# A gated MLP after block-sparse attention: u and the spatial product computed with channels on partitions

## The chip, the cores and the metric

The kernel runs on one core of a Trainium2 chip. The metric is the device time of one execution in microseconds. A core has five engines that run side by side and meet through semaphores: PE (TensorE, the matrix multiplications; its weight loads are listed apart as PEld), DVE (VectorE), ACT (ScalarE), POOL (GpSimd) and SP (SyncE, which here issues nearly all DMAs, in order). Matrix products are written to tiles in PSUM; everything else lives in SBUF.

## The reference, cut to what matters

Block-sparse attention (4 batches, 8 heads, 768 positions, head size 64) makes x, and a gated MLP with a spatial product follows. The change touches the MLP and a few copies in the attention's setup.

```python
scores = scale * np.matmul(q, k.transpose(0, 1, 3, 2))
scores = np.where(mask, scores, -1e9)          # window, first and last block, 3 sampled blocks a row
attn = softmax(scores);  attn_out = np.matmul(attn, v)
x = attn_out.transpose(0, 2, 1, 3).reshape(B, S, H * D)          # (4, 768, 512)

h = np.maximum(x @ w_in, 0.0)                                    # (4, 768, 1024)
u, v = h[..., :512], h[..., 512:]
v_n = (v - mean(v)) / sqrt(var(v) + 1e-6)                        # over the 512 channels
v_s = np.einsum('ts,bsd->btd', w_spatial, v_n) + b_spatial[None, :, None]
out = (u * v_s) @ w_out                                          # (4, 768, 512)
```

## The kernel before

**Attention.** The work is cut into slots, written out by hand. In each slot PE makes the scores of one step (`qk_unit` in the first 36 slots, batch 0; `qk_full` in the 144 after them), ACT takes the exponential, and PE multiplies the exponentials of an earlier slot with v (`av_unit`, `av_full`, seven slots later). The mask is in the matmul: rows 64 to 95 of the tile `kq` hold, next to the 64 rows of each head's keys and queries, one-hot rows of the key's block and the query block's penalties. `rows` copies these from head 0 to others, and `mask_rows` makes the penalties by a small matmul of `bm`. In the setup one of the copies for head 2 (`rows(slice(2, 3), ...)`) is done by ACT (512 columns) and one by POOL (256). `filler` issues matmuls on a tile of zeros between the first real ones.

**MLP.** One `Moe` object per batch makes a list of steps, one matmul each, and `run_queue` deals them out over the slots: so many behind each slot's scores and attention products. `in_steps` are the products x w_in: per chunk of 128 positions (six, `tcc`) a `v_product` and a `u_product` of four matmuls, with 128 columns of `xt` (x transposed, channels on partitions) as weights and 512 columns of `w_in_t` streamed, so positions are on the output's partitions. v is normalised along its row: DVE takes statistics (`bn_stats`, `bn_aggr`), POOL makes `rstd` for a group of two or three chunks, and `vn_one` lets DVE normalise one chunk, at the earliest 9 steps after the group's statistics and then every second step. The spatial products (`s_product`, six matmuls) have blocks of `w_spt` as weights and stream `vn[:, s, :]` for s = 0 to 5; DVE reads the product from PSUM, adds the bias (`b_col`, one number per partition) and multiplies by u, in place in `un`, in one instruction. The output product needs the gated values with channels on partitions, so they are transposed: `dma_start_transpose` from SP into `gt`, two chunks at a time; for the last batch also one chunk at a time, and the last chunk on PE (`g_transpose`, four transposes and a DVE copy). `o_product` then has `gt` as weights and streams `w_out_t`; ACT or DVE copies the result to `osb`, and SP writes it out.

Batch 0's steps start in slots 16, 29 and 41, those of batches 1 and 2 where their last head ends, and those of batch 3 (`last`, the tail) run after the last slot with nothing between them; there `last_x` begins the products before the last x is complete. A product's PSUM bank comes from two (`moeA`, `moeB`) in turn; in the tail from six. Steps of one batch are in the order written, so what a step waits for on PE holds up all that follows it on PE.

The order of u and v products: `SEQ` for batches 1 and 2, a string in `last_x` for batch 3.

Of the kernel before, what the change touches and what calls it, by code (L numbers as in the profile page):

```python
# [10 lines left out]
FP32 = mybir.dt.float32  # L11
# [15 lines left out]
def kernel(  # L27
# [38 lines left out]
    FILL, FILL2, FILL3 = 26, (2, 2, 2), 3  # L66
# [12 lines left out]
    b_col = const.tile([128, NCH], FP32)  # L79
# [129 lines left out]
    def dve_copy(o, i):  # L209
        nc.vector.tensor_copy(out=o, in_=i)  # L210
# [76 lines left out]
    filler(FILL2[0], wps)  # L287
    mask_rows(psum.tile([128, 1024], FP32, tag="sc", bufs=2, name="mq"), 0, act_copy, 1)
    rows(slice(2, 3), slice(0, 512), nc.scalar)
    filler(FILL2[1], wps)  # L290
# [4 lines left out]
    filler(FILL2[2], wps)  # L295
    mask_rows(psum.tile([128, 512], FP32, tag=moe_tag(), bufs=1, name="mq"), 1, act_copy, rs=MR)
    split0(psq, 0, *Q4, 1)
    rows(H1, qcols(0, 2), PL)
    rows(slice(2, 3), slice(512, S), PL)
# [22 lines left out]
    nc.sync.dma_start(out=b_col, in_=moe_b_spatial.rearrange("(p c) -> p c", c=NCH))  # L322
# [198 lines left out]

    def ws_cast(i):
        if i % 2 == 0:
            ws["b", i // 2] = work.tile([128, 2, NCH, 128], BF16, tag="ws_b", bufs=2, name="ws_b")
        src = ws.pop(("f", i)).rearrange("p (s c) -> p c s", c=NCH)
        for c0 in range(0, NCH, NCH // 3):
            cs = slice(c0, c0 + NCH // 3)
            nc.gpsimd.tensor_copy(out=ws["b", i // 2][:, i % 2, cs], in_=src[:, cs])
# [36 lines left out]
    class Moe:  # L565
        def __init__(self, b):
            self.b, self.last = b, b == B - 1
            w = lambda nm: work.tile([128, NCH, DH], BF16, tag=nm, bufs=1, name=nm)
            self.un, self.vn = w("un"), w("vn")
            self.gt = work.tile([128, NCH, NDH, 128], BF16, tag="gt", bufs=1, name="gt")  # L570
            self.mv = work.tile([128, NCH, 2], FP32, tag="mv", bufs=2)
            self.std = work.tile([128, NCH], FP32, tag="std", bufs=2)
            self.rstd = work.tile([128, NCH], FP32, tag="rstd", bufs=2)
            self.vn_due = deque()
            self.steps = 0
# [36 lines left out]
        def u_product(self, tcc):  # L612
            def done(ps):
                if self.b == 0 and tcc in U_DVE:
                    ts(self.un[:, tcc, :], ps, 0.0, ALU.max)
                else:
                    nc.scalar.activation(out=self.un[:, tcc, :], in_=ps, func=AF.Relu)
            return product(NDM, lambda g: self.xt(g, tcc), lambda g: w_in_t[:, g, 0:DH],
                           self.last, done)

        def s_product(self, tcc):
            def done(ps):
                nc.vector.scalar_tensor_tensor(out=self.un[:, tcc, :], in0=ps,  # L623
                                               scalar=b_col[:, tcc:tcc + 1],
                                               in1=self.un[:, tcc, :], op0=ALU.add,
                                               op1=ALU.mult)
                if self.last and tcc == NCH - 1:
                    return
                if self.last and tcc == NCH - 2:
                    g0 = tcc  # L630
                elif tcc % 2 == 1:
                    g0 = tcc - 1
                else:
                    return
                nc.sync.dma_start_transpose(
                    out=self.gt[:, g0:tcc + 1].rearrange("p t c n -> p (t c) n"),
                    in_=self.un[:, g0:tcc + 1, :].rearrange("p t d -> p (t d)"))
            return product(NCH, lambda s: w_spt[:, tcc, s, :], lambda s: self.vn[:, s, :],
                           self.last, done)


        def g_transpose(self):
            ps = bank("ps_g", "av")
            for d in range(NDH):
                tr(ps, d, self.un[:, NCH - 1, d * 128:(d + 1) * 128])
            dve_copy(self.gt[:, NCH - 1].rearrange("p c n -> p (c n)"), ps[:, 0:NDH * 128])

        def o_product(self, tcc, n):
# [4 lines left out]
            for i in range(parts):  # L653
# [10 lines left out]
                steps += product(NDH, lambda d: self.gt[:, tcc, d, :],  # L664
# [9 lines left out]
        def rest_steps(self):  # L674
            out = []
            for tcc in range(NCH):
                out += self.s_product(tcc)
            first = out[0]
            out[0] = lambda: ([self.vn_one(True) for _ in range(NCH)], first())
            for n, tcc in enumerate((0, 1, 5, 2, 3, 4) if self.last else range(NCH)):  # L680
                out += self.o_product(tcc, n)
                if self.last and n == 1:
                    out.insert(len(out) - 3, self.g_transpose)
            return out
# [29 lines left out]
    ROWS = [(3, 2, 8, qcols(0)), (1, 3, 4, K_), (4, 4, 6, K_), (8, 6, 8, K_),  # L714
# [54 lines left out]
    def last_x():  # L769
# [4 lines left out]
        seq = m.in_steps("v0 v1 u0 v2 v3 v4 v5 u1 u2 u3 u4 u5", 3)  # L774
# [41 lines left out]
    for i, sl in enumerate((24, 30, 50)):  # L816
        when(sl, c(ws_tr, i))
    when(50, *[c(w_out_load, g) for g in range(NDH)])
# [61 lines left out]
```

## Time and profile before

| | |
|---|---|
| median of 3 runs | 210.97 us (210.81 to 211.08) |
| the profiled execution | 211.73 us, of which the span 209.9 us |
| setup, until ACT's exponentials run without a gap | 0 to 12.5 us |
| batch 0's attention (36 slots) | to about 47 us |
| batches 1 to 3's attention (144 slots), the MLP of batches 0 to 2 between | to about 182 us |
| the tail: MLP of batch 3 | 182 to 206.4 us, then the last write |

The profile lists each engine's busy time, the groups of instructions by line, operation and tiles, what each waited for, the chain that ended last, and timelines by engine with start and duration. Its times are those of one execution; matmuls are pipelined, so a group's mean duration (378 ns for 512 columns) is a latency, and the distance of two starts (216 ns) is what one costs in a row. A small part of the matmul records is missing from the trace.

### The profile page before, as it was taken

To read this page: it belongs to the slowest core of one execution; us is meant where nothing else is said; L and a number is where in the kernel's file an instruction comes from. 1 tells how busy PE (TensorE), PEld (TensorE's weight loads), DVE (VectorE), ACT (ScalarE), POOL (GpSimd) and SP (SyncE) were. 2 spreads that over 40 slices of the span, in tenths; PEclk is the share of its full clock that TensorE was granted. 3 is DMA by queue.
4 is the path that set the end of the run, shared out by engine and by line. 5 is a ranking of instruction groups with operands and counts; after the bars stand their busy time and mean duration, and the time that the engine had idled before them with its cause. 6 is when DMAs were issued, how large, how long until landed. Compare 5 with 4: busy or idle time off the path is not lost.

```text
span 209.9 us, 5319 instructions
## 1 busy us (share of the span) xinstructions
PE 201.3 (96%) x2106; PEld 129.1 (61%) x2140; DVE 136.4 (65%) x301; ACT 168.8 (80%) x222; POOL 83.3 (40%) x184
## 2 busy tenths in 40 slices
PE   8789999999999999999999999999999999999993
PEld 6569878766666666665566556665566556544441
DVE  7768987999874756484975454284985443476551
ACT  6979999999999999979998888979889787266021
POOL 6689869957828726006159051006220000012000
PEclk9999999999999999999999999999999999999998
DMA  5999799999999999999965497478501225610256
GB/s 162 330 357 344 222 314 285 251 301 359 250 338 188 264 165 296 270 219 345 210 216 112 116 247 179 153 177 262 102 3 35 53 53 116 222 54 0 50 146 228
DMA packets 64684, 41.96 MB, mean 200 GB/s; under 512 B 45716, under 2 KB 59412, under 8 KB 64660
## 3 DMA queue, kind: packets, MB, share of 16 engines
q1 hardware_dynamic: 64228, 41.24, 76.0%
q10 hardware_dynamic: 432, 0.39, 0.6%
q8 instruction: 16, 0.26, 0.5%
q14 instruction: 8, 0.07, 0.1%
HBM read 24.38 MB, written 6.29 MB: 146 GB/s over the span
## 4 chain that ended last, share of the span: by engine, by line
PE 87%; DMA 4%; DVE 2%; SPq 1%; ACT 1%; issue 1%; POOL 0%; ACTq 0%
PE ps_moe L555 31%; PE ps L421 22%; PE ps_av L469 13%; PE ps_t L555 7%; PE ps L408 6%; PE ps_av L451 4%; DMA st_k<-in_k_dram 4%; PE ps_sc L555 3%; PE ps L262 1%; SPq L108 1%; DVE kq L210 1%; ACT a_all L413 1%; DMA out_dram<-osb 1%; PE ps_av L262 1%; ACT osb L213 0%
## 5 line engine op out<-in xcount | busy, mean ns | idle before, releaser
L424 ACT ACTIVATE a_all<-ps 128x768 bf16<-128x768 f32 x144 | 113.7, 811 | 15.5 <-PE ps L421 7.2
L421 PE MATMUL ps<-kq 128*128 128x512 bf16 (+1 forms) x288 | 70.3, 325 | 0.2
L469 PEld LDWEIGHTS <-a_all 128*128 128x128 bf16 x864 | 46.6, 98 | 19.4
L469 PE MATMUL ps_av<-vv,a_all 128*128 128x65 bf16 x864 | 51.0, 194 | 0.1
L421 PEld LDWEIGHTS <-kq 128*128 128x128 bf16 x288 | 27.8, 97 | 30.1 <-issue 0.2
L555 PE MATMUL ps_moe<-w_in_t,xt 128*128 128x512 bf16 x128 | 39.4, 378 | 0.5
L413 ACT ACTIVATE a_all<-ps 128x1024 bf16<-128x1024 f32 x35 | 33.9, 1024 | 1.9 <-PE ps L408 1.4
L136 POOL CAST nat<-st_k 128x256 bf16<-128x256 f32 (+3 forms) x37 | 16.7, 482 | 42.9 <-DMA st_k<-in_k_dram 31.4
L555 PE MATMUL ps_moe<-vn,w_spt 128*128 128x512 bf16 x98 | 30.5, 378 | 0.6
L592 POOL TENSOR_SCALAR std<-mv 128x3 f32<-128x3 f32 (+1 forms) x9 | 2.1, 238 | 50.8 <-DVE mv L589 36.9
L408 PE MATMUL ps<-kq 88*128 88x256 bf16 (+1 forms) x136 | 21.0, 275 | 1.0 <-DVE kq L210 0.6
L623 DVE SCALAR_TENSOR_TENSOR un<-ps_moe,b_col,un 128x512 bf16<-128x512 f32 x18 | 13.5, 748 | 12.9 <-PE ps_moe L555 10.9
L555 PE MATMUL ps_moe<-w_out_t,gt 128*128 128x512 bf16 x66 | 20.2, 378 | 0.1
L555 PEld LDWEIGHTS <-xt 128*128 128x128 bf16 x192 | 15.2, 97 | 7.1 <-DVE xt L210 0.2
L433 DVE RECIPROCAL rc<-ps_av 128x6 f32<-128x6 f32 (+1 forms) x36 | 6.6, 184 | 19.9 <-PE ps_av L469 18.8
L434 DVE TENSOR_TENSOR xn<-ps_av,rc 128x384 bf16<-128x384 f32 (+1 forms) x36 | 18.5, 513 | 1.2
L136 POOL CAST nat<-st_q 128x256 bf16<-128x256 f32 (+2 forms) x41 | 17.2, 447 | 3.9 <-DMA st_q<-in_q_dram 3.6
L136 POOL CAST vv<-st_v 128x256 bf16<-128x256 f32 (+1 forms) x36 | 17.4, 516 | 3.1 <-DMA st_v<-in_v_dram 3.0
L588 DVE BATCH_NORM_STATS2 stats<-vn 128x6 f32<-128x512 bf16 x24 | 16.5, 688 | 1.5 <-ACT vn L583 0.9
L184 DVE TENSOR_SCALAR vn<-ps_moe 128x512 bf16<-128x512 f32 x18 | 12.3, 683 | 6.0 <-PE ps_moe L555 6.0
L451 PE MATMUL ps_av<-vv,a_all 128*128 128x65 bf16 x288 | 14.6, 194 | 1.0 <-POOL vv L136 1.0
L451 PEld LDWEIGHTS <-a_all 128*128 128x128 bf16 x288 | 13.5, 98 | 2.7 <-issue 1.5
(92 smaller groups left out, 215.5 us busy)
## 6 DMA issues: line engine op xcount, KB each, us to landing
st_v<-in_v_dram SPq DMA_DIRECT2D x16, 384.0 KB, 6.0
out_dram<-osb SPq DMA_DIRECT2D x23, 256.0 KB, 2.4
st_k<-in_k_dram SPq DMA_DIRECT2D x15, 384.0 KB, 4.4
st_q<-in_q_dram SPq DMA_DIRECT2D x12, 384.0 KB, 4.9
ws_f<-in_moe_w_spatial_dram SPq DMA_DIRECT2D x6, 384.0 KB, 4.7
w_f<-in_moe_w_in_dram SPq DMA_DIRECT2D x8, 256.0 KB, 5.6
w_f<-in_moe_w_out_dram SPq DMA_DIRECT2D x4, 256.0 KB, 5.6
st_q<-in_q_dram SPq DMA_DIRECT2D x3, 256.0 KB, 6.9
```

The source lines that it names most:

```text
L136: eng.tensor_copy(out=dst, in_=src)
L184: nc.vector.tensor_scalar(out=out, in0=in0, scalar1=s1, scalar2=s2, op0=o0, **kw)
L408: nc.tensor.matmul(out=ps[:, at:at + n * TW], lhsT=kq[0:KR, h, ci * 128:(ci + 1) * 128], rhs=kq[0:KR, h, qcols(t0, n)], start=True, stop=True)
L413: nc.scalar.activation(out=out, in_=ps, func=AF.Exp, scale=0.125)
L421: nc.tensor.matmul(out=ps[:, n0:n1], lhsT=kq[:, j % H, ci * 128:(ci + 1) * 128], rhs=kq[:, j % H, S + n0:S + n1], start=True, stop=True)
L424: nc.scalar.activation(out=a_ref["h", j][:, ci, :], in_=ps[:, 0:S], func=AF.Exp, scale=0.125)
L434: nc.vector.tensor_tensor(out=out, in0=ps[:, :, 0:D], in1=rc[:, 0:n].to_broadcast([128, n, D]), op=ALU.mult)
L451: nc.tensor.matmul(out=av_ref[u][:, to, :], lhsT=a_ref[u][:, at:at + 128], rhs=vv[pp % NVV][:, h, ci, :], start=(ci == 0), stop=(ci == NCH ...
L469: nc.tensor.matmul(out=av_ref[j][:, qc, :], lhsT=a_ref["h", j][:, ci, qc * 128:(qc + 1) * 128], rhs=vv[p % NVV][:, h, ci, :], start=(ci == ...
L555: nc.tensor.matmul(out=ref["ps"][:, 0:w], lhsT=lhs(i), rhs=rhs(i), start=(i == 0), stop=(i == n - 1))
L588: nc.vector.bn_stats(out=stats, in_=self.vn[:, tcc, :])
L623: nc.vector.scalar_tensor_tensor(out=self.un[:, tcc, :], in0=ps, scalar=b_col[:, tcc:tcc + 1], in1=self.un[:, tcc, :], op0=ALU.add, op1=AL ...
```

## The change

The u product and the spatial product swap their two operands. u: 128 columns of `w_in_t` (channels) are the weights and `xt` (positions) is streamed; spatial: 128 channels of `vn[:, s, :]` are the weights and the rows of `w_spt` are streamed. Both results then have channels on partitions. Each product fills one bank of 512 numbers, as an area of `nd` blocks of channels by `n` chunks of positions: for u in batch 0 two blocks by two chunks; in the other batches two blocks by the first two chunks (products 0, 1) and one block by the last four (2 to 5); for the spatial products one block by the first four chunks (0 to 3) and two blocks by the last two (4, 5). With nd = 2 a product is made of twice as many matmuls of 256 columns, two to a step; the number of steps is the same. `un` holds the gated values as [channel, block of channels, position] and is the output product's weights itself; `gt`, its transposes and `g_transpose` are gone, and the last batch's output chunks run in order.

The bias now runs along the free dimension: `b_load` brings it on SP in slot 46 as a broadcast to all 128 partitions (the small load of `b_col` in the setup goes), a DVE copy in slot 52 puts it in the order of the chunks (`b_row`), and the eviction is two DVE instructions, an add into the float32 tile `sb` and a multiply by u.

The last batch's order of products is v0 v1 v2 u0 ... instead of v0 v1 u0 v2 ...; in the setup, four fillers stand behind both mask products in place of two at each of three places, and head 2's key rows are copied by DVE in slot 0 instead of by ACT and POOL ahead of it.

```diff
@@ -63,7 +63,7 @@
     TC = NCH // NT
     TW = TC * 128
     S0 = NT * NG * 3
-    FILL, FILL2, FILL3 = 26, (2, 2, 2), 3
+    FILL, FILL2, FILL3 = 26, 4, 3
     U_DVE = (0, 1, 2, 3, 4, 5)
 
     const = ctx.enter_context(tc.tile_pool(name="const", bufs=1))
@@ -76,7 +76,7 @@
     w_in_t = const.tile([128, NDM, DFF], BF16)
     w_out_t = const.tile([128, NDH, DM], BF16)
     w_spt = const.tile([128, NCH, NCH, 128], BF16)
-    b_col = const.tile([128, NCH], FP32)
+    b_row = const.tile([128, S], FP32)
     mhalf = const.tile([128, NCH], FP32)
 
     kq = const.tile([128, H, 2 * S], BF16, name="kq")
@@ -284,19 +284,15 @@
     ps0 = bank()
     head(ps0, 0, *K4)
     split0(ps0, 0, *K4, 0)
-    filler(FILL2[0], wps)
     mask_rows(psum.tile([128, 1024], FP32, tag="sc", bufs=2, name="mq"), 0, act_copy, 1)
-    rows(slice(2, 3), slice(0, 512), nc.scalar)
-    filler(FILL2[1], wps)
     psq = bank("psq", "av")
     head(psq, 0, *Q4)
     split0(psq, 0, *Q4, 0)
     split0(ps0, 0, *K4, 1)
-    filler(FILL2[2], wps)
     mask_rows(psum.tile([128, 512], FP32, tag=moe_tag(), bufs=1, name="mq"), 1, act_copy, rs=MR)
+    filler(FILL2, wps)
     split0(psq, 0, *Q4, 1)
     rows(H1, qcols(0, 2), PL)
-    rows(slice(2, 3), slice(512, S), PL)
 
     ORDER = ("k1 q1a v0 k2 q2a v1 k3 q3a v2 q1b q2b r v3 q3b q0c w00 w01 w02 w03 w10 w12 w11 w13").split()
     PIECE = {"k": ALLC, "v": ALLC, "a": C01, "b": C25, "c": C45, "q": ALLC}
@@ -319,7 +315,6 @@
             rows(slice(2, 4), qcols(1), PL)
         for y in ORDER[i + AHEAD:i + AHEAD + 1]:
             ahead(y)
-    nc.sync.dma_start(out=b_col, in_=moe_b_spatial.rearrange("(p c) -> p c", c=NCH))
 
     def second():
         ps2 = bank("ps2", "av")
@@ -519,6 +514,10 @@
         nc.sync.dma_start(out=ws["f", i],
                           in_=moe_w_spatial.rearrange("(p c) s -> c p s", c=NCH)[i])
 
+    def b_load():
+        ws["b_nat"] = work.tile([128, S], FP32, tag="ws_f", bufs=6, name="b_nat")
+        nc.sync.dma_start(out=ws["b_nat"], in_=moe_b_spatial.partition_broadcast(128))
+
     def ws_cast(i):
         if i % 2 == 0:
             ws["b", i // 2] = work.tile([128, 2, NCH, 128], BF16, tag="ws_b", bufs=2, name="ws_b")
@@ -566,8 +565,8 @@
         def __init__(self, b):
             self.b, self.last = b, b == B - 1
             w = lambda nm: work.tile([128, NCH, DH], BF16, tag=nm, bufs=1, name=nm)
-            self.un, self.vn = w("un"), w("vn")
-            self.gt = work.tile([128, NCH, NDH, 128], BF16, tag="gt", bufs=1, name="gt")
+            self.vn = w("vn")
+            self.un = work.tile([128, NDH, S], BF16, tag="un", bufs=1, name="un")
             self.mv = work.tile([128, NCH, 2], FP32, tag="mv", bufs=2)
             self.std = work.tile([128, NCH], FP32, tag="std", bufs=2)
             self.rstd = work.tile([128, NCH], FP32, tag="rstd", bufs=2)
@@ -609,41 +608,56 @@
                 ts(self.vn[:, tcc, :], self.vn[:, tcc, :], self.mv[:, tcc, 0:1], ALU.subtract,
                    self.rstd[:, tcc:tcc + 1], ALU.mult)
 
-        def u_product(self, tcc):
+        def in_place(self, d0, nd, c0, n):
+            return self.un[:, d0:d0 + nd, c0 * 128:(c0 + n) * 128]
+
+        def by_columns(self, k, d0, nd, c0, n, lhs, rhs, done):
+            ref, out = {}, []
+            mms = [(x, i) for x in range(nd) for i in range(k)]
+
+            def run(j):
+                if j == 0:
+                    ref["ps"] = moe_ps(self.last)
+                for x, i in mms[j * nd:(j + 1) * nd]:
+                    o = ref["ps"][:, x * n * 128:(x + 1) * n * 128]
+                    nc.tensor.matmul(out=o.rearrange("p (c t) -> p c t", c=n),
+                                     lhsT=lhs(i)[:, (d0 + x) * 128:(d0 + x + 1) * 128],
+                                     rhs=rhs(i), start=(i == 0), stop=(i == k - 1))
+                if j == k - 1:
+                    done(ref["ps"][:, 0:512].rearrange("p (d t) -> p d t", d=nd))
+            return [lambda j=j: run(j) for j in range(k)]
+
+        def u_product(self, i):
+            if self.b == 0:
+                area = (2 * (i % 2), 2, TC * (i // 2), TC)
+            else:
+                area = (2 * i, 2, 0, 2) if i < 2 else (i - 2, 1, 2, NCH - 2)
+            d0, nd, c0, n = area
+
             def done(ps):
-                if self.b == 0 and tcc in U_DVE:
-                    ts(self.un[:, tcc, :], ps, 0.0, ALU.max)
+                if self.b == 0 and i in U_DVE:
+                    ts(self.in_place(*area), ps, 0.0, ALU.max)
                 else:
-                    nc.scalar.activation(out=self.un[:, tcc, :], in_=ps, func=AF.Relu)
-            return product(NDM, lambda g: self.xt(g, tcc), lambda g: w_in_t[:, g, 0:DH],
-                           self.last, done)
-
-        def s_product(self, tcc):
+                    nc.scalar.activation(out=self.in_place(*area), in_=ps, func=AF.Relu)
+            return self.by_columns(
+                NDM, *area, lambda g: w_in_t[:, g, 0:DH],
+                lambda g: xt_ref[self.b * NG + g][:, c0 * 128:(c0 + n) * 128].rearrange(
+                    "p (c t) -> p c t", c=n), done)
+
+        def s_product(self, i):
+            area = (i, 1, 0, NCH - 2) if i < NDH else (2 * (i - NDH), 2, NCH - 2, 2)
+            d0, nd, c0, n = area
+
             def done(ps):
-                nc.vector.scalar_tensor_tensor(out=self.un[:, tcc, :], in0=ps,
-                                               scalar=b_col[:, tcc:tcc + 1],
-                                               in1=self.un[:, tcc, :], op0=ALU.add,
-                                               op1=ALU.mult)
-                if self.last and tcc == NCH - 1:
-                    return
-                if self.last and tcc == NCH - 2:
-                    g0 = tcc
-                elif tcc % 2 == 1:
-                    g0 = tcc - 1
-                else:
-                    return
-                nc.sync.dma_start_transpose(
-                    out=self.gt[:, g0:tcc + 1].rearrange("p t c n -> p (t c) n"),
-                    in_=self.un[:, g0:tcc + 1, :].rearrange("p t d -> p (t d)"))
-            return product(NCH, lambda s: w_spt[:, tcc, s, :], lambda s: self.vn[:, s, :],
-                           self.last, done)
-
-
-        def g_transpose(self):
-            ps = bank("ps_g", "av")
-            for d in range(NDH):
-                tr(ps, d, self.un[:, NCH - 1, d * 128:(d + 1) * 128])
-            dve_copy(self.gt[:, NCH - 1].rearrange("p c n -> p (c n)"), ps[:, 0:NDH * 128])
+                sb = work.tile([128, 512], FP32, tag="sb", bufs=2, name="sb").rearrange(
+                    "p (d t) -> p d t", d=nd)
+                nc.vector.tensor_tensor(
+                    out=sb, in0=ps, op=ALU.add,
+                    in1=b_row[:, None, c0 * 128:(c0 + n) * 128].to_broadcast([128, nd, n * 128]))
+                nc.vector.tensor_tensor(out=self.in_place(*area), in0=sb,
+                                        in1=self.in_place(*area), op=ALU.mult)
+            return self.by_columns(NCH, *area, lambda s: self.vn[:, s, :],
+                                   lambda s: w_spt[:, c0:c0 + n, s, :], done)
 
         def o_product(self, tcc, n):
             steps = []
@@ -661,7 +675,7 @@
                     (nc.scalar if i else nc.sync).dma_start(
                         out=out[self.b].rearrange("(p c) d -> c p d", c=NCH)[tcc][:, cs],
                         in_=osb["t"][:, cs])
-                steps += product(NDH, lambda d: self.gt[:, tcc, d, :],
+                steps += product(NDH, lambda d: self.un[:, d, tcc * 128:(tcc + 1) * 128],
                                  lambda d, cs=cs: w_out_t[:, d, cs], self.last, done, w)
             return steps
 
@@ -677,10 +691,8 @@
                 out += self.s_product(tcc)
             first = out[0]
             out[0] = lambda: ([self.vn_one(True) for _ in range(NCH)], first())
-            for n, tcc in enumerate((0, 1, 5, 2, 3, 4) if self.last else range(NCH)):
-                out += self.o_product(tcc, n)
-                if self.last and n == 1:
-                    out.insert(len(out) - 3, self.g_transpose)
+            for n in range(NCH):
+                out += self.o_product(n, n)
             return out
 
     queue = deque()
@@ -711,7 +723,7 @@
         return lambda: f(*a, **kw)
 
     K_Q0 = slice(0, S + TW)
-    ROWS = [(3, 2, 8, qcols(0)), (1, 3, 4, K_), (4, 4, 6, K_), (8, 6, 8, K_),
+    ROWS = [(0, 2, 3, K_), (3, 2, 8, qcols(0)), (1, 3, 4, K_), (4, 4, 6, K_), (8, 6, 8, K_),
             (15, 4, 6, qcols(1, 2)), (17, 6, 8, qcols(1, 2))]
     when(0, second)
     when(1, third)
@@ -771,7 +783,7 @@
         m = moe[B - 1]
         while queue:
             queue.popleft()()
-        seq = m.in_steps("v0 v1 u0 v2 v3 v4 v5 u1 u2 u3 u4 u5", 3)
+        seq = m.in_steps("v0 v1 v2 u0 v3 v4 v5 u1 u2 u3 u4 u5", 3)
         n = NG - 1
         for i in (0, 1):
             for f in seq[i * NG:i * NG + n]:
@@ -815,6 +827,9 @@
         when(ca, c(ws_cast, i))
     for i, sl in enumerate((24, 30, 50)):
         when(sl, c(ws_tr, i))
+    when(46, b_load)
+    when(52, lambda: nc.vector.tensor_copy(out=b_row.rearrange("d (c p) -> d c p", c=NCH),
+                                           in_=ws.pop("b_nat").rearrange("d (p c) -> d c p", c=NCH)))
     when(50, *[c(w_out_load, g) for g in range(NDH)])
     when(58, *[c(w_out_cast, g, PL) for g in range(NDH)])
 
```

## The prediction

> **What bounds the kernel now.** First the whole span: busy time by engine, and the chain that ended last, added up by engine.
>
> ```profile
> PE 201.3 (96%) x2106; PEld 129.1 (61%) x2140; DVE 136.4 (65%) x301; ACT 168.8 (80%) x222; POOL 83.3 (40%) x184
> ...
> PE 87%; DMA 4%; DVE 2%; SPq 1%; ACT 1%; issue 1%; POOL 0%; ACTq 0%
> ```
>
> PE (TensorE) carries 87% of the chain. The windows of ten microseconds say how full it is: 9.89 of 10.00 in nearly all from 50 to 190 us. The missing 0.11 is one hole of 0.2 us every 5.04 us, always where a product matmul should stand; the table of groups has 128 of the 144 u and v matmuls of batches 0 to 2 and 98 of 108 spatial ones, so the holes are missing records and PE is never idle there. What PE waits for in that stretch is therefore lost to the end, and what DVE (VectorE) or the queues save in it is worth nothing. Two places decide: slot 52, where batch 0's spatial products begin, and the tail after 190 us. Around slot 52 I read the timelines of DVE, SP's queue and PE (start, duration, engine), then the time to landing of loads issued there:
>
> ```profile
> 54.46 1.38 DVE L184 TENSOR_SCALAR un<-ps_moe 128x512 bf16<-128x512 f32 x2
> 55.76 0.89 DVE L184 TENSOR_SCALAR vn<-vn,mv,rstd 128x512 bf16<-128x512 bf16 x2
> 57.35 0.20 DVE L433 RECIPROCAL rc<-ps_av 128x6 f32<-128x6 f32 x1 [0.69 <-PE ps_av L469]
> ...
> 47.74 4.16 SPq L367 DMA_TRANSPOSE tt<-nat  x1
> 51.95 0.64 SPq L108 DMA_DIRECT2D st_k<-in_k_dram  x1
> ...
> 57.88 0.59 PE L555 MATMUL ps_moe<-vn,w_spt 128*128 128x512 bf16 x2
> ...
> st_k<-in_k_dram SPq DMA_DIRECT2D x1, 384.0 KB, 5.7
> ```
>
> DVE normalises v's last two chunks (vn 4 and 5) from 55.76 to 56.65 us; PE's first spatial product reads them at 57.88 and 58.10. The slack is 1.2 us. The load issued on SP at 51.95 landed 5.7 us later. In the tail (all engines):
>
> ```profile
> 188.45 0.88 POOL L594 TENSOR_TENSOR rstd<-std,mhalf 128x3 f32<-128x3 f32 x1
> 188.75 0.66 DVE L588 BATCH_NORM_STATS2 stats<-vn 128x6 f32<-128x512 bf16 x1
> 189.55 0.70 DVE L184 TENSOR_SCALAR vn<-vn,mv,rstd 128x512 bf16<-128x512 bf16 x2
> 190.17 0.69 DVE L588 BATCH_NORM_STATS2 stats<-vn 128x6 f32<-128x512 bf16 x1
> 191.54 0.88 POOL L594 TENSOR_TENSOR rstd<-std,mhalf 128x3 f32<-128x3 f32 x1
> 192.46 1.06 DVE L184 TENSOR_SCALAR vn<-vn,mv,rstd 128x512 bf16<-128x512 bf16 x3 [1.09 <-POOL rstd L594]
> 192.91 2.75 PE L555 MATMUL ps_t<-vn,w_spt 128*128 128x512 bf16 x12
> 200.68 1.24 PE L555 MATMUL ps_t<-w_out_t,gt 128*128 128x512 bf16 x5
> 202.67 3.36 PEld L555 LDWEIGHTS <-gt 128*128 128x128 bf16 x20 [0.36 <-DVE gt L210]
> ```
>
> A chain DVE statistics, POOL rstd, DVE normalise runs just ahead of PE: vn 3 to 5 are ready at 192.84, 193.18 and 193.52, and PE (216 ns a matmul) reads them at 193.56, 193.77 and 193.99. The slack is 0.5 us.
>
> **The change, part by part.**
>
> *Gated values no longer transposed.* In the middle, nine DMA transposes leave SP's queue (1.2 to 2.5 us of SP each); they are in no chain share, so nothing. SP's loads behind them go earlier, but their readers are POOL's casts, and POOL has 0% of the chain. In the tail the output products run from 200.68 to 206.32; 24 matmuls at 216 ns are 5.18 and the last one's latency adds 0.06, so 0.40 of it is the four PE transposes and the wait for `gt`: **-0.4**. Bounds -0.45 to -0.3.
>
> *More matmuls of half the width.* Streamed columns stay the same. Pairs of 256 in place of one 512: u 24 (batch 0) + 3x8, spatial 4x12 = 96 pairs. A 256 with its own weights costs 109 ns (the final halves: (0.60-0.272)/3) to 110 (QK's four in 0.44), a 512 costs 216: 2.7 to 4 ns a pair, 0.26 to 0.38: **+0.3**. The spatial products now stream w_spt in runs of 128 columns 1,536 bytes apart; no row shows such a read. If nothing, 0; if each run cost like a matmul of its own (transposes of 128: 56 ns, four are 224), 8 ns for each of the 96 wide ones and 4 for each of the 96 half-wide: +1.1. No gain is possible, the columns being the same. I take 0, as each run is as contiguous as the reads shown.
>
> *Spatial eviction in two DVE instructions.* 750 ns become an add from PSUM (rows: 424 ns for 256 elements, 557 for 384, so 690 for 512) and a multiply of a float32 by a bfloat16 tile in SBUF, which no row shows: between 439 (tensor-scalar on 512 bf16) and 750; I take 650, as float32 passes lie near the upper end. So +0.59 each, 14 us of DVE in all. Six add 3.5 us to the stretches 59 to 76, 112 to 127 and 160 to 176 us, where DVE is busy 10.97, 8.30 and 7.49 us: hidden by DVE's idle time before each (1.0 us typical). Uncovered, a bank would be late by at most 0.6 us; it is wanted again only two products (5.7 us) later. In the tail 1.34 against PE's 1.30 a product: the last result falls 0.3 us further behind, yet lands near 203.1, and its first reader, output chunk 4, comes at about 204.8. **0.**
>
> *The bias row.* The small b_col load (3 KB) leaves the queue. A 384 KB broadcast load of the bias is put on SP at slot 46, behind the tt transpose and ahead of st_k, so at 51.9 us; and a DVE copy of 128x768 float32 at slot 52, in DVE's order between the two un evictions (done at 55.84) and the normalising of vn 4 and 5. Landing: st_k, st_q, st_v landed at 57.65, 58.6 and 59.7, about 1.0 us apart, behind the transpose that landed at 56.5 (47.74 + 8.8). The bias takes st_k's turn: 57.6. Bounds: the 4.1 us median of st_k gives 56.0, the slowest st_k, 8.3, gives 60.2. The copy: between 0.42 (a copy of 64x512 bf16) and 0.95 (512 float32 from PSUM, 688 ns, carried on at 1.04 ns); a memset of 768 four-byte elements took 0.70, which I take. Then DVE is through at 58.35, vn 5 at 59.25, and PE reads it 0.1 later at 59.35, not 58.10: **+1.3**. Bounds 0 (landed by 56.0, vn 5 ready at 57.7) to +3.8. Queued behind the waiting copy on DVE: vn, the av normalise (57.35), the memset, the kq split (59.08), whose readers are 4 us off or more. The loads behind the bias on SP land 1 us later; w_spt's third part lands near 62 and is read near 69.
>
> By the Trainium skill ("VectorE: DVE Perf Modes", the perf-mode tier table) a float32 copy within SBUF runs at two elements a cycle, which by that page's formula would be an estimated 0.56 us, and the sum 0.14 lower; its page "SBUF — State Buffer" charges steps beyond 16 bytes, and this copy reads every 24, which speaks for more. No row here shows either.
>
> *The last batch's order v0 v1 v2 u0.* As built, DVE's order becomes stats 0 to 3, normalise 0 and 1, stats 4, normalise 2, stats 5; before, stats 4 stood ahead of both normalisings. Stats 3 ends with its aggregate at 188.83; normalising must wait for POOL's rstd, 188.45 + 0.88 = 189.33 (v2's statistics keep their place, as DVE takes all in a row from 185.54). So 189.4 normalise x2 (0.62 to the next), stats 4 at 190.0, normalise 2 at 190.8, stats 5 at 191.1 in place of 190.17, aggregate done at 192.0, rstd at 193.35 (POOL's two took 1.26 + 0.1), vn 3 to 5 at 193.75, 194.1 and 194.45. PE reads vn 5 at 194.6, not 193.99: **+0.6**. Bounds 0 (0.5 us of slack) to +0.9.
>
> *Setup.* ACT's row copy (0.61) and POOL's (0.39) go; DVE does it in 0.35 at slot 0, in the 0.70 it idles before 6.91; six fillers become four. The first exponential could start at 5.35, not 5.46. But PE stands 1.04 us at 11.36 for vv (POOL had waited 1.56 for that load, issued at 3.56, whose place stays) and ACT 1.00 at 12.51: everything meets there again. **0**; bounds -0.6 (ACT's copy, passed on) to +0.35 (DVE's, uncovered).
>
> Sum: -0.4 + 0.3 + 1.3 + 0.6 = +1.8 on a profiled span of 209.9 us, 1.83 more of which lies around it (211.73). The median of the runs, 210.97, is 0.8 below the profiled run; I add the same 1.8: **212.8**.
>
> **The rivals.** *The bias is there in time* (landed by 56.0): no wait at slot 52, +0.5, 211.5. For it: typical st_k loads need 4.1 us. Against: two loads and a transpose of this stretch needed 5.7 to 8.8.
>
> *PE has slack* (the other side): if the 0.2 us holes were idle time, PE would have 0.04 us to catch up per microsecond, 1.3 us within 33 us; both the wait at slot 52 and the half-wide matmuls vanish, leaving the tail's +0.2, 211.2, not slower by what can be measured. It decides from one hole in three being real. Against: the counts above.
>
> *Setup passes through, the bias in time, the tail's wait at its lower bound 0:* -0.4 + 0.3 - 0.6 = -0.7, 210.3. Against: the waits at 11.36 and 12.51.
>
> *Strided streaming costs:* +1.1 on top, 213.9.
>
> **How the numbers follow.** Forecast 0.56, bias in time 0.24, slack 0.05, setup 0.07, strided 0.08. Below 0.2% (0.42 us) a measurement of this kernel can't tell a difference. Faster: setup 0.07 and 0.05 of the bias case at its low bounds, 0.12. Same: slack 0.05 and 0.10 of the bias case, 0.15. Slower: the rest, 0.73. Range: from 210.7 (into the bias case's low half) to 213.9 (strided, or a landing 1 us later still), leaving out 2 in 10. The forecast's own: 212.1 to 213.5.
>
> **What would show it.** A DVE idle of 1 us or more before the b_row copy, put down to the DMA, and PE idle near 58 us before a weight load of vn; in the tail a weight load of vn waiting for DVE near 194 us, and no stop between output products. Spatial matmuls at 216 and 109 ns. ACT's wait near 12.5 us unchanged. Wrong, if PE shows no idle at both vn waits.

## The result, and the profile after

The changed kernel takes 213.78 us in the median (211.84 to 214.34), the one before 211.09 us on the same chip (210.81 to 211.90): a ratio of 1.0108 [1.0083, 1.0134], some 2.3 us slower. The ratio is not the quotient of the two medians, which differ by 2.7 us; in what follows the ratio counts. Runs over 1.5% above the fastest of their kernel are in the medians and not in the ratios. The prediction was 212.8 us in a range of 210.7 to 213.9, "slower" with 0.73. The profiled execution took 213.72 us with a span of 211.9 us, against 211.73 and 209.9 before: 2.0 us more, and these 2.0 us are what can be placed.

First the page of the changed kernel: busy time by engine, the chain that ended last, and the two groups of the new eviction (busy us, mean ns, idle time before).

```profile
PE 203.8 (96%) x2230; PEld 138.5 (65%) x2230; DVE 153.5 (72%) x326; ACT 168.3 (79%) x221; POOL 85.7 (40%) x183
...
PE 82%; DVE 8%; DMA 4%; ACT 2%; POOL 1%; issue 1%; POOLq 0%; ACTq 0%; SPq 0%
...
L657 DVE TENSOR_TENSOR un<-sb,un 128x512 bf16<-128x512 f32 x24 | 17.0, 709 | 1.5
...
L654 DVE TENSOR_TENSOR sb<-ps_moe,b_row 128x512 f32<-128x512 f32 x18 | 12.4, 687 | 5.4 <-PE ps_moe L623 5.1
```

DVE has 17 us more work, and PE is still the bound, but DVE's share of the chain went from 2% to 8% and PE's from 87% to 82%: somewhere PE now waits for DVE. Two places in the timeline show where. Around slot 52 (start, duration, engine; in brackets the idle time before an instruction and what ended it), and then the bias load's row among the issues, with its time to landing:

```profile
52.64 0.59 SPq L519 DMA_DIRECT2D b_nat<-in_moe_b_spatial_dram  x1
...
54.78 0.69 DVE L184 TENSOR_SCALAR un<-ps_moe 128x512 bf16<-128x512 f32 x1 [0.24 <-PE ps_moe L623]
...
56.78 0.38 PE L623 MATMUL ps_moe<-w_spt,vn 128*128 128x512 bf16 x1
...
57.32 0.35 PE L464 MATMUL ps_av<-vv,a_all 128*128 128x65 bf16 x6
57.61 1.34 DVE L831 COPY b_row<-b_nat 128x768 f32<-128x768 f32 x1 [2.13 <-DMA b_nat<-in_moe_b_spatial_dram]
58.87 0.72 DVE L184 TENSOR_SCALAR vn<-vn,mv,rstd 128x512 bf16<-128x512 bf16 x2
59.33 0.10 PEld L623 LDWEIGHTS <-vn 128*128 128x128 bf16 x1 [1.78 <-DVE vn L184]
59.33 0.71 PE L623 MATMUL ps_moe<-w_spt,vn 128*128 128x512 bf16 x2 [1.66 <-DVE vn L184]
```

```profile
b_nat<-in_moe_b_spatial_dram SPq DMA_DIRECT2D x1, 384.0 KB, 5.0
```

Read it from the bottom up. PE's fifth spatial matmul stands 1.66 us for vn 4. DVE had nothing to do for 2.13 us before that, but its next instruction in order was the copy of the bias row, whose load was issued at 52.64 and landed 5.0 us later, at 57.6. The normalising stood behind that copy, although its rstd had been there since 53.4 and DVE free since 55.5.

In the tail (all engines):

```profile
190.14 0.88 POOL L593 TENSOR_TENSOR rstd<-std,mhalf 128x3 f32<-128x3 f32 x1
...
191.05 0.74 DVE L184 TENSOR_SCALAR vn<-vn,mv,rstd 128x512 bf16<-128x512 bf16 x2 [0.53 <-POOL rstd L593]
...
191.70 0.69 DVE L587 BATCH_NORM_STATS2 stats<-vn 128x6 f32<-128x512 bf16 x1
...
192.82 0.69 DVE L587 BATCH_NORM_STATS2 stats<-vn 128x6 f32<-128x512 bf16 x1
...
194.13 0.88 POOL L593 TENSOR_TENSOR rstd<-std,mhalf 128x3 f32<-128x3 f32 x1
...
194.63 3.22 PE L623 MATMUL ps_t<-w_spt,vn 128*128 128x512 bf16 x12
195.05 1.06 DVE L184 TENSOR_SCALAR vn<-vn,mv,rstd 128x512 bf16<-128x512 bf16 x3 [1.32 <-POOL rstd L593]
195.51 0.10 PEld L623 LDWEIGHTS <-vn 128*128 128x128 bf16 x1 [0.57 <-DVE vn L184]
```

DVE idles 0.53 us for POOL's first rstd with the fourth chunk's statistics still to do behind the normalising; statistics, second rstd and the last three normalisings are late by that, and the first twelve spatial matmuls take 3.22 us where the kernel before took 2.75.

The 2.0 us, place by place, in the two profiled executions (start in the one before, start after, difference):

| landmark on PE | before | after | difference |
|---|---|---|---|
| first scores of batch 1 (slot 36) | 41.72 | 41.35 | -0.37 |
| scores behind the pair of matmuls that reads vn 4 and 5 | 58.31 | 59.88 | +1.57 |
| tail, first v product | 182.22 | 183.91 | +1.69 |
| tail, first spatial product | 192.91 | 194.63 | +1.72 |
| tail, first output product | 200.68 | 202.90 | +2.22 |
| end of the last output product | 206.32 | 208.25 | +1.93 |

The stop at slot 52 is thus worth 1.94, the one in the tail 0.47 to 0.50, the output products without PE's transposes give back 0.29, and the long stretch between, with all its half-width matmuls, costs 0.12. From the start of slot 36 to the end of the last output product the changed kernel takes 166.90 us and the one before 164.60, 2.30 more; the lead of 0.37 lies ahead of that, where executions differ whatever the kernel (slot 36 begins between 40.25 and 41.72 us over all the kernels profiled).

### The profile page after: what moved, and what is told of

It reads as the page before. It is cut to its first block, busy times and chain, and to the rows that moved or that the text cites. A ratio compares the mean times of both kernels' runs of the same rounds, so it can differ in the third digit from the quotient of the medians.

```text
span 211.9 us, 5524 instructions
## 1 busy us (share of the span) xinstructions
PE 203.8 (96%) x2230; PEld 138.5 (65%) x2230; DVE 153.5 (72%) x326; ACT 168.3 (79%) x221; POOL 85.7 (40%) x183
## 4 chain that ended last, share of the span: by engine, by line
PE 82%; DVE 8%; DMA 4%; ACT 2%; POOL 1%; issue 1%; POOLq 0%; ACTq 0%; SPq 0%
PE ps L416 20%; PE ps_moe L623 17%; PE ps_moe L554 14%; PE ps_av L464 12%; PE ps L403 6%; PE ps_av L446 4%; PE ps_t L554 3%; DMA b_nat<-in_moe_b_spatial_dram 2%; PE ps_t L623 2%; DVE stats L587 2%; DVE kq L210 2%; DVE vn L184 2%; DMA st_q<-in_q_dram 2%; ACT a_all L408 1%; PE ps_sc L623 1%; PE ps L262 1%
## 5 line engine op out<-in xcount | busy, mean ns | idle before, releaser
L464 PEld LDWEIGHTS <-a_all 128*128 128x128 bf16 x864 | 46.6, 98 | 19.4
L464 PE MATMUL ps_av<-vv,a_all 128*128 128x65 bf16 x864 | 51.0, 194 | 0.0
L623 PE MATMUL ps_moe<-w_spt,vn 128*128 128x512 bf16 (+1 forms) x144 | 32.9, 325 | 1.7 <-DVE vn L184 1.7
L623 PE MATMUL ps_moe<-xt,w_in_t 128*128 128x256 bf16 (+1 forms) x112 | 22.8, 302 | 0.0
L554 PE MATMUL ps_moe<-w_in_t,xt 128*128 128x512 bf16 x72 | 22.3, 378 | 0.1
L554 PE MATMUL ps_moe<-w_out_t,un 128*128 128x512 bf16 x72 | 21.5, 378 | 0.0
L623 PEld LDWEIGHTS <-vn 128*128 128x128 bf16 x192 | 15.5, 97 | 7.0 <-DVE vn L184 3.0
L136 POOL CAST vv<-st_v 128x256 bf16<-128x256 f32 (+1 forms) x36 | 19.1, 565 | 1.0 <-DMA st_v<-in_v_dram 0.8
L657 DVE TENSOR_TENSOR un<-sb,un 128x512 bf16<-128x512 f32 x24 | 17.0, 709 | 1.5
L654 DVE TENSOR_TENSOR sb<-ps_moe,b_row 128x512 f32<-128x512 f32 x18 | 12.4, 687 | 5.4 <-PE ps_moe L623 5.1
L428 DVE RECIPROCAL rc<-ps_av 128x6 f32<-128x6 f32 (+1 forms) x36 | 6.6, 184 | 13.3 <-PE ps_av L464 12.5
```

The source lines that it names most:

```text
L136: eng.tensor_copy(out=dst, in_=src)
L464: nc.tensor.matmul(out=av_ref[j][:, qc, :], lhsT=a_ref["h", j][:, ci, qc * 128:(qc + 1) * 128], rhs=vv[p % NVV][:, h, ci, :], start=(ci == ...
L554: nc.tensor.matmul(out=ref["ps"][:, 0:w], lhsT=lhs(i), rhs=rhs(i), start=(i == 0), stop=(i == n - 1))
L623: nc.tensor.matmul(out=o.rearrange("p (c t) -> p c t", c=n), lhsT=lhs(i)[:, (d0 + x) * 128:(d0 + x + 1) * 128], rhs=rhs(i), start=(i == 0) ...
L657: nc.vector.tensor_tensor(out=self.in_place(*area), in0=sb, in1=self.in_place(*area), op=ALU.mult)
```

## Experiments

Times of the kernel before are from the same chip and the same rounds as each group: 211.31 us for the early load, the copy in arrival order, the later normalising and the order alone; 211.16 us for the other four. The changed kernel was not run again in these rounds, so it is compared by the ratios.

**The bias loaded thirteen slots earlier** (from the changed kernel):

```diff
-    when(46, b_load)
+    when(33, b_load)
```

> The changed kernel with the bias load on SP in slot 33 instead of 46, the DVE copy still in slot 52. If PE lost 1.9 us because the copy waited 2.1 us for the load and vn 4 and 5 stood behind it on DVE: the load lands near 51 us, the copy runs from 55.5 to 56.85, vn 5 is ready at 57.6, PE's idle before a weight load of vn near 58 us is at most 0.2 us, and the time falls by 1.7 to 1.9 to about 212.0. If PE has slack, or the extra 384 KB themselves cost the time, it stays near 213.8.

Measured: 211.53 us, ratio 1.0016 [0.9989, 1.0043]. Its timeline, DVE and PE:

```profile
54.96 0.85 DVE L831 COPY b_row<-b_nat 128x768 f32<-128x768 f32 x1
...
55.74 0.89 DVE L184 TENSOR_SCALAR vn<-vn,mv,rstd 128x512 bf16<-128x512 bf16 x2
...
57.05 0.59 PE L623 MATMUL ps_moe<-w_spt,vn 128*128 128x512 bf16 x2
```

No bracket: the copy waits for nothing, and PE goes on at 57.05 in step with the scores around it. Some 2 us of the loss are gone with a load moved and nothing else. Had PE had slack in this stretch, the kernel could not have gained from it. The same 384 KB are still loaded and the same copy is still made on DVE, so neither the traffic nor DVE's extra work had cost the time. The time is below the 212.0 expected. The tail's stop is still there (its first twelve spatial matmuls take 3.22 us): from slot 36 to the end this execution takes 164.96 us, 0.36 more than the kernel before, and that is what the other rows of the table add up to. Three of the twelve runs took 213.5 to 214.2 us; they have no trace, and why is not known.

**The copy two slots later, the load where it was** (from the changed kernel):

```diff
-    when(52, lambda: nc.vector.tensor_copy(out=b_row...
+    when(54, lambda: nc.vector.tensor_copy(out=b_row...
```

> The changed kernel with the load still in slot 46 and only the DVE copy moved from slot 52 to 54, so that in DVE's order it stands behind the normalising of vn 4 and 5, the attention's normalising and a memset, and ahead of a kq split and the first spatial eviction. If the cost is what stands behind the waiting copy (vn 4 and 5, which PE reads near 57.7 us), and not the wait or the load: DVE may still wait for the load, PE doesn't stop, and the time is as with the early load, 211.5 to 212.0. If the late eviction of the first spatial product or the late kq split takes the place of the stop, it stays above 213.

Measured: 211.20 us, ratio 1.0010 [0.9983, 1.0037]; one of the twelve runs took 213.62 us. Its timeline:

```profile
54.46 0.98 DVE L184 TENSOR_SCALAR vn<-vn,mv,rstd 128x512 bf16<-128x512 bf16 x2
...
56.53 0.59 PE L623 MATMUL ps_moe<-w_spt,vn 128*128 128x512 bf16 x2
...
57.73 0.86 DVE L831 COPY b_row<-b_nat 128x768 f32<-128x768 f32 x1
```

The load landed at 56.5 here, after the normalising was done, and nothing stopped; the copy itself did not have to wait any more. Together the two say what the cost was: not the load, not the copy, but an instruction that PE needs standing in DVE's order behind one that waits.

**The copy in arrival order** (from the changed kernel):

```diff
-    when(52, lambda: nc.vector.tensor_copy(out=b_row.rearrange("d (c p) -> d c p", c=NCH),
-                                           in_=ws.pop("b_nat").rearrange("d (p c) -> d c p", c=NCH)))
+    when(52, lambda: nc.vector.tensor_copy(out=b_row, in_=ws.pop("b_nat")))
```

> The changed kernel with the DVE copy in slot 52 reading the bias in the order it arrives (the reordering by chunk is left out). If the copy's 1.34 us come from reading every 24 bytes: it takes 0.5 to 0.7, everything behind it is 0.65 to 0.85 earlier, and the time falls by as much, to 213.0 to 213.1. If 768 float32 elements take 1.34 in any order, or the wait for the load hides it, it stays at 213.8.

Measured: 212.53 us, ratio 1.0056 [1.0027, 1.0084]. Its timeline:

```profile
56.23 0.73 DVE L831 COPY b_row<-b_nat 128x768 f32<-128x768 f32 x1 [0.67 <-DMA b_nat<-in_moe_b_spatial_dram]
...
56.88 0.88 DVE L184 TENSOR_SCALAR vn<-vn,mv,rstd 128x512 bf16<-128x512 bf16 x2
...
57.60 0.60 PE L623 MATMUL ps_moe<-w_spt,vn 128*128 128x512 bf16 x2
```

The copy took 0.73 us. Reading every 24 bytes thus cost up to 0.6 us in the changed kernel's execution (1.34), and as little as 0.1 in others (last section). The ratio fell by 0.5%, some 1.1 us, which is more than expected, with intervals that just touch, and this profiled execution shows no stop at all: SP issued the load at 50.72, it landed 5.5 us later at 56.2, and PE was in time. One profile can't say how often that is so; a median 1.2 us above the kernel before says that it is not the rule. So both when the load is issued and how long the copy takes set the cost; this run doesn't tell their shares apart.

**The last batch's normalising due four steps later** (from the changed kernel; the fourth chunk's statistics then stand ahead of it on DVE):

```diff
-                        self.vn_due.extend((t, self.steps + VN_AGE + VN_STEP * i)
+                        self.vn_due.extend((t, self.steps + (13 if self.last else VN_AGE) + VN_STEP * i)
```

> The changed kernel with the last batch's first normalising allowed 13 steps after its statistics instead of 9, which puts DVE's order in the tail back to statistics 4, normalise 0 and 1, statistics 5, normalise 2. If PE's stop in the first spatial product of the tail comes from statistics 4 standing behind a normalising that waits for POOL: vn 5 is ready 0.9 us earlier, the stop is gone, and the time falls by 0.5, to 213.3. If the two-instruction evictions or the product order itself cost it, it stays at 213.8.

Measured: 213.18 us, ratio 1.0089 [1.0057, 1.0121], 0.4 us below the changed kernel's, with intervals that overlap. The profiled execution was the longest of the twelve, 216.85 us, as PE stopped for 3.23 us at slot 52 and its clock fell behind that (last section). In the tail the clock is at 1.00 again, and only the order there is compared:

```profile
194.84 0.70 DVE L184 TENSOR_SCALAR vn<-vn,mv,rstd 128x512 bf16<-128x512 bf16 x2
195.47 0.69 DVE L587 BATCH_NORM_STATS2 stats<-vn 128x6 f32<-128x512 bf16 x1
...
196.84 0.88 POOL L593 TENSOR_TENSOR rstd<-std,mhalf 128x3 f32<-128x3 f32 x1
...
198.23 2.75 PE L623 MATMUL ps_t<-w_spt,vn 128*128 128x512 bf16 x12
```

The first normalising waits for nothing, the second rstd starts 1.39 us ahead of PE's first spatial matmul (0.50 in the changed kernel), and the twelve take 2.75 us: the stop is gone.

**That order alone in the kernel before:**

```diff
-        seq = m.in_steps("v0 v1 u0 v2 v3 v4 v5 u1 u2 u3 u4 u5", 3)
+        seq = m.in_steps("v0 v1 v2 u0 v3 v4 v5 u1 u2 u3 u4 u5", 3)
```

> The kernel before with nothing changed but the last batch's order v0 v1 v2 u0. If the order alone makes the late normalising: PE stops before the fourth to sixth matmul of the first spatial product, and the time rises by 0.4 to 0.6, to 211.5 to 211.7. If it needs the exchanged operands (vn as weights), it stays at 211.1.

Measured: 211.35 us, ratio 1.0008 [0.9987, 1.0029]. Its timeline in the tail:

```profile
189.19 0.74 DVE L184 TENSOR_SCALAR vn<-vn,mv,rstd 128x512 bf16<-128x512 bf16 x2 [0.52 <-POOL rstd L594]
...
192.74 3.23 PE L555 MATMUL ps_t<-vn,w_spt 128*128 128x512 bf16 x12
193.18 1.06 DVE L184 TENSOR_SCALAR vn<-vn,mv,rstd 128x512 bf16<-128x512 bf16 x3 [1.32 <-POOL rstd L594]
```

The stop is there with the old operands too, to a hundredth: 0.52 on DVE, 3.23 on PE. So it belongs to the order and not to the swapped product. The time is below the 211.5 to 211.7 expected, and by it a loss of 0.5 us is neither shown nor excluded; the interval reaches from -0.3 to +0.6 us. The traces show it: from slot 36 to the end this execution takes 165.14 us, 0.54 more than the kernel before, and 0.46 more than that kernel with the new setup (next experiment).

**The setup edit alone, in the kernel before, and the changed kernel without it.** Here a part of the change that had been costed at nothing is added and taken away:

```diff
-    FILL, FILL2, FILL3 = 26, (2, 2, 2), 3
+    FILL, FILL2, FILL3 = 26, 4, 3
...
-    rows(slice(2, 3), slice(0, 512), nc.scalar)
...
-    rows(slice(2, 3), slice(512, S), PL)
...
-    ROWS = [(3, 2, 8, qcols(0)), (1, 3, 4, K_), (4, 4, 6, K_), (8, 6, 8, K_),
+    ROWS = [(0, 2, 3, K_), (3, 2, 8, qcols(0)), (1, 3, 4, K_), (4, 4, 6, K_), (8, 6, 8, K_),
```

> The kernel before with the setup edit alone. If it is worth nothing: 211.1 to 211.4, no difference from the kernel before. If it is worth the 0.4 us by which the changed kernel was ahead at 47 us: 210.8.

> The changed kernel with the setup as before (two fillers at three places, head 2's key rows by ACT and POOL in the setup). If the setup edit is worth nothing, as all engines meet again at the loads near 9 to 12 us: 213.5 to 213.9, and ACT's first exponential at 5.5 to 6.1 us depending on when the first q load lands. If the 0.4 us by which the changed kernel was ahead at 47 us came from the setup edit: 214.2.

Measured: alone 211.00 us, ratio 1.0008 [0.9980, 1.0037]: no difference shown, with room for -0.4 to +0.8 us. From slot 36 to the end that execution takes 164.68 us against 164.60. The changed kernel without it took 214.54 us in six runs, ratio 1.0138 [1.0092, 1.0184], above both expectations, with an interval that overlaps the changed kernel's. Its timeline at slot 52 shows why its median is no measure of the setup:

```profile
55.87 0.38 PE L627 MATMUL ps_moe<-w_spt,vn 128*128 128x512 bf16 x1
...
57.91 1.03 DVE L835 COPY b_row<-b_nat 128x768 f32<-128x768 f32 x1 [3.34 <-DMA b_nat<-in_moe_b_spatial_dram]
58.85 0.82 DVE L184 TENSOR_SCALAR vn<-vn,mv,rstd 128x512 bf16<-128x512 bf16 x2
...
59.41 0.96 PE L627 MATMUL ps_moe<-w_spt,vn 128*128 128x512 bf16 x2 [2.65 <-DVE vn L184]
```

PE came to this place 0.9 us sooner than in the changed kernel (55.87 against 56.78) and left it at the same time (59.41 against 59.33), since the landing sets when it goes on. A lead won before slot 52 was worth nothing in this execution, and the longer stop had a price of its own (last section).

**The change with both stops taken away.** The load in slot 33, the copy in slot 45 by POOL, the last batch's normalising due four steps later (from the changed kernel):

```diff
-    when(46, b_load)
-    when(52, lambda: nc.vector.tensor_copy(out=b_row...
+    when(33, b_load)
+    when(45, lambda: nc.gpsimd.tensor_copy(out=b_row...
...
-                        self.vn_due.extend((t, self.steps + VN_AGE + VN_STEP * i)
+                        self.vn_due.extend((t, self.steps + (13 if self.last else VN_AGE) + VN_STEP * i)
```

> The changed kernel with both waits taken out: bias load in slot 33, its copy by POOL in slot 45, and the last batch's normalising allowed after 13 steps. By the sum of the parts (0.3 more for the half-wide matmuls, 0.3 less for the tail's transposes) it should equal the kernel before, 211.0 to 211.4. If strided streaming or the evictions cost something that the two stops hid, it is slower by 0.5 or more; if the transposes' DMA traffic had cost something, it is faster by 0.5 or more.

Measured: 210.84 us (210.05 to 211.60), ratio 0.9980 [0.9961, 0.9999]. Its timeline at slot 52:

```profile
52.13 1.58 POOL L831 COPY b_row<-b_nat 128x768 f32<-128x768 f32 x1 [1.54 <-DMA b_nat<-in_moe_b_spatial_dram]
...
55.36 1.45 DVE L184 TENSOR_SCALAR vn<-vn,mv,rstd 128x512 bf16<-128x512 bf16 x2
...
57.37 0.59 PE L623 MATMUL ps_moe<-w_spt,vn 128*128 128x512 bf16 x2
```

POOL waited for the load in DVE's place. The rstd of chunks 4 and 5 stood behind it there, and still the normalising was done at 56.81, 0.6 us before PE's pair. In its tail the twelve spatial matmuls took 2.75 us. By the two ratios this version is ahead of the changed kernel by 1.3%; ahead of the kernel before it is by 0.2%, with an interval that ends just short of 1. In its trace the stretch from slot 36 to the end takes 164.61 us, as in the kernel before (164.60). So the swap of operands itself costs nothing on balance: what the changed kernel lost lay in three things beside it, where the load is issued, where the copy stands, and the order v0 v1 v2 u0.

## Why the prediction was right

**The bias row (+1.3 forecast).** The mechanism was as told: the copy waits for the landing, vn 4 and 5 stand behind it, PE waits for these. Both tests that take it away (an earlier load, a later copy) bring the time back to 211.2 to 211.5 us. The size is off: 1.57 against the kernel before's schedule, and 1.94 against the changed kernel's own, as it came to slot 52 with a lead of 0.37. The landing was forecast for 57.6 and came at 57.6, but that was luck, two errors that cancel: the load was issued at 52.64 and not 51.9, because SP's transpose ahead of it took 5.24 us and not 4.16, and it landed after 5.0 us and not 5.7. The term that was mis-sized is the copy: 1.34 us, above the upper bound of 0.95. The rows that bounded it are of elements that lie side by side, and the copy reads one in six; in arrival order it took 0.73, near the 0.70 that was chosen. The Trainium skill ("SBUF — State Buffer", the note on cachelines in "Door 1: The DMA port swizzle") charges for steps beyond 16 bytes without a price; here the direction of that is right, and the estimate of 0.56 from the Trainium skill's page "VectorE: DVE Perf Modes" (the perf-mode tier table) is too low even for the copy in arrival order. Of the 0.64 by which the copy was longer, 0.3 reached PE, as the two normalisings behind it took 0.72 and not 0.89 and began 0.08 before its recorded end.

**The order v0 v1 v2 u0 (+0.6 forecast).** Right, instruction by instruction: DVE's idle time for the rstd, statistics 4 behind it, a weight load of vn waiting for DVE. PE lost 0.47 in place of 0.6. In the measured times alone it couldn't be told from nothing; that it is real rests on the traces of the changed kernel, of the order with the old operands (the stop is there), and of the new operands with a later due time (it is gone).

**Gated values no longer transposed (-0.4).** Right in kind, a little large: from the first output product to the end 5.35 us in place of 5.64, so -0.29. This is what the whole change gains.

**Half-width matmuls (+0.3), strided streaming (0).** In the tail twelve starts of the spatial products, six of them by pairs, take 2.61 us against 2.59: about 3.3 ns a pair (the 0.02 us is at the limit of what the view resolves), within the 2.7 to 4 forecast. Streaming w_spt in runs of 128 columns 1,536 bytes apart costs nothing that shows: 378 ns a matmul, as before, and 2.75 us for twelve in a row where no stop stands between them. The rival that priced each run falls.

**Two-instruction eviction (0).** The add took 687 ns (690 forecast), the multiply 709 (650): the row that reads PSUM was the nearer one, not the tensor-scalar. Hidden all the same: the version with both stops taken away has all 24 pairs and is no slower than the kernel before.

**Setup (0).** No run contradicts it, but its reason held for one execution only. The first exponential was to start at 5.35 us and not 5.46; it started at 6.04, as ACT idles 0.71 for the second mask product. That product was late because the first q load had come late in this execution: POOL's cast of it began at 4.44, against 3.81 before (POOL's and ACT's timelines of the changed kernel):

```profile
4.44 0.40 POOL L136 CAST nat<-st_q 128x256 bf16<-128x256 f32 x1 [1.06 <-DMA st_q<-in_q_dram]
...
5.48 0.37 ACT L213 ACTIVATE kq<-mq 32x256 bf16<-32x256 f32 x1 [0.71 <-PE mq L268]
6.04 0.60 ACT L398 ACTIVATE a_all<-ps 128x512 bf16<-128x512 f32 x1 [0.19 <-PE ps L395]
...
7.01 7.91 ACT L408 ACTIVATE a_all<-ps 128x1024 bf16<-128x1024 f32 x8
```

Over all the profiles the first exponential starts between 5.43 and 6.04 us with the new setup and between 5.46 and 6.10 with the old one, so no effect of the edit shows. And ACT's wait near 12.5, which was to stay, is not in the changed kernel's profile: ACT runs without a gap from 7.01. It is absent too from two profiles with the old setup, the changed kernel without the edit and the order alone, so the setup edit is not its cause. Before, POOL had begun to cast the first load of v at 10.48, after a wait of 1.56; in the other nine profiles that cast begins between 8.37 and 9.63. The meeting of all engines near 12 us, from which the 0 was argued, thus goes with the late load of that one execution.

**The rivals.** PE has no slack: the earlier load gained some 2 us. "The bias is there in time" (211.5) is what the earlier load was made to be, and it measured 211.53. Among the changed kernel's own times one, 211.84, lies where that rival would put it; whether the load was in time in that execution isn't known, as it has no trace.

The sum was +1.8; the profiled executions differ by 2.0, the ratio gives 2.3, as does the stretch from slot 36 on. That the sum came within 0.2 of the profiled executions is in part luck: the stop at slot 52 was 0.6 longer than forecast, and a lead of 0.37 that nothing had forecast took most of that back. How long the stop would have been without the lead was not settled.

## What to carry to other kernels

Where PE is full, a new instruction on a helper engine costs its wait before it costs its length, and it charges both to whatever stands behind it in that engine's order: list what that is, and who needs it when. A load that is read once has its place slots ahead of its reader, not just ahead; if its landing can't be relied on, the reader goes behind the work that PE needs, or on an engine that PE doesn't wait for. And a reordering of matmuls reorders the helper engines too: check which instruction now stands behind a wait there.

## What the runs showed of the hardware

**Behind a longer stop of PE its clock was halved.** The windows of two microseconds (window; its length, busy us and instructions of PE, PEld, DVE, ACT, POOL; granted clock; DMA share; GB/s), first of the changed kernel, whose stop was 1.66 us, then of the one with the old setup, whose stop was 2.65 us:

```profile
58.00:60.00 2.00, 0.67 (x3) 0.31 (x4) 1.97 (x5) 0.36 (x1) 0.26 (x1) 1.00 1.37 358
60.00:62.00 2.00, 2.00 (x26) 1.28 (x24) 1.75 (x4) 1.54 (x2) 0.00 (x0) 1.00 1.68 177
```

```profile
58.00:60.00 2.00, 0.59 (x2) 0.26 (x3) 1.97 (x5) 0.00 (x0) 1.20 (x2) 0.88 1.15 366
60.00:62.00 2.00, 2.00 (x12) 0.95 (x11) 1.75 (x4) 0.81 (x1) 0.00 (x0) 0.50 1.70 173
62.00:64.00 2.00, 2.00 (x20) 1.30 (x19) 1.71 (x3) 1.12 (x2) 0.00 (x0) 0.77 0.62 163
```

The clock stays at 1.00 in the first; in the second it is down to 0.50 for some 3.4 us (an estimate from the three windows: 0.5 + 2.0 + 0.9), and PE gets 12 instructions through where the first has 26. PE went on only 0.08 us later in the second, yet its first spatial matmul of the tail starts 1.61 us later (196.24 against 194.63): a microsecond more of stop cost another 1.5 us behind it. All of it is lost within four microseconds: the scores behind PE's next pair of spatial matmuls start at 63.17 against 61.56, the same 1.61 us later. In the execution of 216.85 us (the later normalising) the stop was 3.23 us and the clock 0.50 for some 6.8, by the same estimate (0.8 + 6.0 + 0.04). The other times fit this: of the six runs with the old setup the three longest, 215.3 to 216.4 us, the profiled one among them, have a mean granted clock of 0.991, and the other three, 213.0 to 213.8 us, one of 0.998 to 0.999. The Trainium skill ("TensorE: Matmul & The Clock Gate", Part 1) gives the half rate after an idle window of about 3.4 us; the half rate agrees, but here a wait of 2.65 us was enough. Between 1.66 and 2.65 us nothing was tried.

**The length of one strided copy varies.** The same 128x768 float32 copy with a read step of 24 bytes took 0.85 and 0.86 us where it ran without a wait, and 1.03, 1.05 and 1.34 where it began as its load landed; in POOL's hands it took 1.58. What it shares with the transfers around it was not tried.
